# A condition vector loaded as one row and a planner's limits as a table, in an adaLN transformer block on one core

## The chip, the core and the metric

The kernel runs on one core of a Trainium2 chip. A core has five engines with queues of their own: TensorE (PE) multiplies matrices into PSUM, VectorE (DVE) and ScalarE (ACT) read PSUM and work elementwise, GpSimd (POOL) works on SBUF alone, SyncE (SP) only issues DMAs here. ACT and POOL issue DMAs too. The metric is the device time of one execution in microseconds.

## The reference

One block with adaptive layer norm: 2048 tokens, width 512, 32 heads of 16, a feed-forward part 1376 wide, all in bf16.

```python
mod = (_silu(c) @ w_mod).reshape(c.shape[0], 6, 1, -1)
sa, ca, ga, sb, cb, gb = (mod[:, i] for i in range(6))
h = _layernorm(x) * (1 + ca) + sa
q, k, v = heads(h @ wqkv)
p = _softmax(q @ k^T * Dh ** -0.5)
x = x + ga * ((p @ v) @ wo)
h = _layernorm(x) * (1 + cb) + sb
x = x + gb * (_gelu(h @ w1 + b1) @ w2 + b2)
```

(shortened; `heads` stands for the reshape and transposition into 32 heads.) The condition `c` is one row of 512. Nearly all of the time goes to the softmax: 32 x 2048 x 2048 exponentials.

## The kernel before

**Scored pairs.** The queries are cut into four blocks `b` of 512 tokens, the keys into sixteen tiles `kt` of 128, the heads into eight groups of four, a group being one `quad` with a block. A *scored pair* is one head of a quad with one key tile: a matmul of 32 rows of `kT` with 512 queries (L902, `qk`) makes 128 x 512 scores in one PSUM bank. Four heads lie on the four row groups of PE and run side by side. The last four quads are worked in two halves of 256 queries, where one pair holds two key tiles. There are 2048 pairs in all.

A pair's exponential goes one of two ways. ScalarE does two or three banks at once with Exp (L1379, `exp_to`) into `PB`. Or VectorE makes it out of integer bits: a *fill* (L1523) adds a bias and writes 16-bit integers to `TB`, which read as half floats are a piecewise power of two; two *shifts* (L1557) subtract constants, for two more pieces. Such a pair enters the second matmul three times, once with `VE` (the values) and twice with `VV`, the values scaled by `WJ[1]` and `WJ[2]`, which POOL makes at the start for six of the sixteen key tiles (L308). The second matmul (L1141, `pe_pv`) sums over all key tiles in bank 7; a column of ones gives the denominators. `emit_out` copies bank 7 out (L1472) and sends the denominators through DRAM: `d1` (L1477), back as `dall` with 16 a row (L1479), a reciprocal on VectorE (L1491), out again as `d2` (L1493), back broadcast to `rb` (L1496), and POOL multiplies (L1500). Projections, gating and the feed-forward part of the blocks run between (L435 for most of their matmuls; Gelu on ScalarE at L649 once for each of the first three blocks).

**The planner.** The order of all this work on every engine is written out by a planner that runs while the program is built. It keeps a clock for each engine, a time at which each bank and slot is free, and a due time `rdy[...]` for each result, and it asks the engine whose clock is least for its next step. What it decides is the order on each queue; on the chip an engine takes its instructions in that order and waits where an input isn't there. The limits for its choices come from `TUNE` through `tv(i)`, with one row for each 128 pairs scored (`scored[0] >> 7`), seventeen rows, all alike so far: 0, VectorE takes a further pair while the work waiting for it is under this; 1, the same for taking one outside a burst for ScalarE; 2, PE fills a bank group for ScalarE when ScalarE has less work than this ahead; 3, how far other work on PE may run over that time; 4 and 5, whether a burst waits for a bank that VectorE will soon free; 6, the least heads for which a group of second matmuls is issued early; 7, whether bank 2 is given as a third bank to ScalarE. Where PE has nothing to do the planner lets it multiply by zeros (`pe_idle`, L1222).

`open_late` (L556) is one POOL step: it frees the prologue's memory and issues the loads of `W_1` (L561) and `W_2` (L565) on ACT's queue and small ones on SP's. In `emit_out` the due time of the denominators is that of the copy plus 6000 ns (L1487); the reciprocal is placed in VectorE's order when that time has come.

**The front.** Before the planner starts, a fixed prologue runs: the first block `xb[0]` in four tiles on two queues (L140), `c` on POOL's queue spread over 128 partitions (`cc_bf`, L141: four elements on each, read one at a time), `W_m0` in two halves (L143), sixteen warm-up matmuls with zeros (`turn_over(WARM[0])`, L348), four statistics on VectorE (L353), with `W_k`'s load held until the second of them is done (L355) and SP's other loads behind it. Then come `ln_rstd`, the SiLU of `c` (`silu_c`: Exp on ScalarE, add, reciprocal and multiply on VectorE, L183 to L186), the modulation columns from `W_m0` (L231), norms, transposes (L371), evacuation to `hT` and the first projections of keys and queries (L379). `WARM[1]` isn't used.

Of the kernel before, what the change touches and what calls it, by code (L numbers as in the profile page):

```python
# [12 lines left out]
BF16 = mybir.dt.bfloat16  # L13
FP32 = mybir.dt.float32
# [6 lines left out]
P = 128  # L21
S = 2048
D = 512
F = 1376
H = 32
NC = 4
# [31 lines left out]
POOL_COVER = 1100.0  # L58
LOCK_WAIT = 100.0
TIE = 60.0  # L60
TUNE = ((1900.0, 900.0, 1350.0, 180.0, 400.0, 600.0, 3, 1),) * 17
T_NEED = 1
T_NEXT = 1
T_OPEN = 0.0
ROOT = 1000.0
ROOT_L = 700.0
SPREAD = (0.9, 0.9, 0.65)
WARM = (16, 3)
FRONT = (1200.0, 0.0, 2600.0, 4000.0)
AHEAD = 32  # L70
T_KEEP = 3
# [22 lines left out]
def adaln_block(ctx: ExitStack, tc: tile.TileContext, A_x, A_wqkv, A_wo, B_x, B_w1, B_b1, B_w2, B_b2,  # L94
                c, w_mod, out):
    nc = tc.nc
# [3 lines left out]
    const = ctx.enter_context(tc.tile_pool(name="const", bufs=1))  # L100
# [4 lines left out]
    kT = res.tile([P, NC, S], BF16, name="kT")  # L105
# [29 lines left out]
    still = kT[:, NC - 1, S - 512:S]  # L135
    nc.vector.memset(still, 0.0)
    W_m0 = prom.tile([P, NC, 2 * D], BF16, name="W_m")
    for i, eng in enumerate((nc.sync, nc.scalar)):
        for t in (2 * i, 2 * i + 1):
            eng.dma_start(out=xb[0][:, t, :], in_=x_tok[0][:, t, :])  # L140
    nc.gpsimd.dma_start(out=cc_bf, in_=c.rearrange("o (j p) -> p (o j)", p=P))  # L141
    for i, eng in enumerate((nc.sync, nc.scalar)):
        eng.dma_start(out=W_m0[:, 2 * i:2 * i + 2, :], in_=wm_v[:, 2 * i:2 * i + 2, 0:2 * D])  # L143

# [33 lines left out]
    scf = const.tile([P, NC], FP32, name="scf")  # L178
    scb = prow.tile([P, NC, P], BF16, name="scb")

    def silu_c():
        ce = const.tile([P, NC], FP32, name="ce")
        nc.scalar.activation(out=ce, in_=cc_bf, func=ACT.Exp, scale=-1.0)  # L183
        nc.vector.tensor_scalar(out=ce, in0=ce, scalar1=1.0, scalar2=None, op0=ALU.add)
        nc.vector.reciprocal(out=ce, in_=ce)
        nc.vector.tensor_tensor(out=sc_bf, in0=cc_bf, in1=ce, op=ALU.mult)  # L186
# [159 lines left out]
    def turn_over(n):  # L346
        for _ in range(n):
            nc.tensor.matmul(out=PS[0:32, 6, :], lhsT=zero, rhs=still, start=True, stop=True)  # L348

    turn_over(WARM[0])  # L350
    st0 = pron.tile([P, 12, 6], FP32, name="st1")
    for t in range(4):
        seen = nc.vector.bn_stats(out=st0[:, t, :], in_=xb[0][:, t, :])  # L353
        if t == 1:
            held = nc.sync.dma_start(out=W_k, in_=wqkv_v[:, :, D:2 * D])  # L355
            tc.add_manual_dep(held.ins, seen.ins.name, AFTER, reason="order of loads")
            nc.sync.dma_start(out=W_q, in_=wqkv_v[:, :, 0:D])
            nc.sync.dma_start(out=xb[1], in_=x_tok[1])
            nc.sync.dma_start(out=W_v, in_=wqkv_v[:, :, 2 * D:3 * D])
            for b in range(2, NQB):  # L360
                nc.sync.dma_start(out=xb[b], in_=x_tok[b])
            W_m1 = load_mod(1, nc.sync)
    psm = bk(7, FP32, 16)
    mv0, rs0 = ln_rstd(st0, 4)
    silu_c()
    first_mod_mm(psm)
    turned = [bk(2 + j, BF16) for j in range(NC)]
    for t in range(4):
# [184 lines left out]
    for j in range(NC):  # L553
        op("POOL", 1220.0, gate(lambda: W_o, j, ga_b), ("wo", j), ["ga"] + ([("wo", j - 1)] if j else []))

    def open_late():  # L556
        pro.close()
        lw = ctx.enter_context(tc.tile_pool(name="latew", bufs=1, side="right"))
        W_1 = lw.tile([P, NC, FPAD], BF16, name="W_1")
        nc.gpsimd.memset(W_1[:, :, F:FPAD], 0.0)  # L560
        nc.scalar.dma_start(out=W_1[:, :, 0:F], in_=B_w1.rearrange("(j p) n -> p j n", p=P))  # L561
        W_2 = lw.tile([P, NFC, D], BF16, name="W_2")
        lr = F - (NFC - 1) * P
        nc.gpsimd.memset(W_2[:, NFC - 1, :], 0.0)
        nc.scalar.dma_start(out=W_2[:, 0:NFC - 1, :],  # L565
                            in_=B_w2[0:(NFC - 1) * P, :].rearrange("(j p) n -> p j n", p=P))
        nc.sync.dma_start(out=W_2[0:lr, NFC - 1, :], in_=B_w2[(NFC - 1) * P:F, :])
        b1_bf = lw.tile([P, NFC], BF16, name="b1_bf")
        nc.gpsimd.memset(b1_bf, BIG)
        nc.sync.dma_start(out=b1_bf[:, 0:NFC - 1], in_=B_b1[0:(NFC - 1) * P].rearrange("(j p) -> p j", p=P))  # L570
        nc.sync.dma_start(out=b1_bf[0:lr, NFC - 1:NFC],
                          in_=B_b1[(NFC - 1) * P:F].rearrange("(p o) -> p o", o=1))
        b1c = lw.tile([P, NFC], FP32, name="b1c")
        nc.gpsimd.tensor_copy(out=b1c, in_=b1_bf)
        nc.sync.dma_start(out=W_2[lr:lr + 1, NFC - 1, :], in_=B_b2.rearrange("(o f) -> o f", o=1))
        nc.gpsimd.tensor_scalar(out=W_2[lr:lr + 1, NFC - 1, :], in0=W_2[lr:lr + 1, NFC - 1, :], scalar1=1.0 / BIG,
                                scalar2=None, op0=ALU.mult)
        clk["ACT"] += 120.0
# [883 lines left out]
    def emit_out(qi, t):  # L1462
# [21 lines left out]
            else:  # L1484
                OT[(b, ch)] = otp.tile([P, 512], BF16, name="OT")
        ot = OT[(b, ch)]
        rdy[("dall", qi)] = clk["DVE"] + 6000.0  # L1487

        def back():
            rp = osp.tile([P, 16], FP32, name="rp")  # L1490
# [254 lines left out]
```

## Time and profile before

| what | us |
|---|---|
| median of 3 timed runs (759.68 to 762.66) | 761.05 |
| the profiled execution | 759.09 |
| its span, first to last instruction | 757.2 |
| PE busy | 737.4 |
| ACT busy | 720.6 |
| DVE busy | 701.0 |
| POOL busy | 110.6 |

In the profile's rows a group reads: line, engine, operation, output <- input, shapes, count, then busy time and mean duration in ns, then the engine's idle time just before and what ended it. A timeline row begins with its start and its length in microseconds, and "x3" means three instructions merged. A row of a stretch gives its bounds and length, then busy time and count for each engine, the granted clock of TensorE as a share of full speed, the DMA engines' busy share and GB/s. A row of the chain of waits gives start, length and what the chain ran through.

### The profile page before, as it was taken

What the parts mean: (1) busy time and instruction counts of PE and PEld (TensorE: products, weight loads), DVE (VectorE), ACT (ScalarE), POOL (GpSimd) and SP (SyncE); (2) the same over time, 40 slices, a digit from 0 to 9 for tenths busy, and PEclk for the clock granted to TensorE, in tenths of its full rate; (3) what the DMA queues carried; (4) which work ended last, traced back from release to release, by engine and by line L of the source; (5) the groups of instructions that cost most, each with busy time, mean ns of one, the idle gap of its engine ahead of it and who ended that gap; (6) DMA issues with size and microseconds to landing.
All of it is one profiled execution on the core that took longest, in us unless ns stands there. A gap on an engine that the chain in (4) does not pass through costs nothing.

```text
span 757.2 us, 21449 instructions
## 1 busy us (share of the span) xinstructions
PE 737.4 (97%) x8885; PEld 259.4 (34%) x8888; DVE 701.0 (93%) x1455; ACT 720.6 (95%) x732; POOL 110.6 (15%) x137
## 2 busy tenths in 40 slices
PE   6999999999899999999999999999999999999997
PEld 3432333233233333223332232332233322444444
DVE  4966999999799999999999999999999999999984
ACT  1999999999899999999999999999999999999993
POOL 3334100211032311101001110100101110010010
PEclk8999999999999999999999999999999999999999
DMA  8300000000500100000001000000001000000000
GB/s 281 109 2 3 16 5 11 7 10 21 148 10 9 38 9 3 10 9 10 17 13 48 10 10 9 10 6 24 22 11 51 10 24 10 17 22 14 5 9 31
DMA packets 27960, 20.49 MB, mean 27 GB/s; under 512 B 14049, under 2 KB 23906, under 8 KB 27858
## 3 DMA queue, kind: packets, MB, share of 16 engines
q1 hardware_dynamic: 25442, 15.57, 7.2%
q10 hardware_dynamic: 2384, 3.51, 1.5%
q8 instruction: 71, 1.16, 0.6%
q14 instruction: 31, 0.25, 0.1%
q0 software_dynamic: 32, 0.00, 0.0%
HBM read 16.45 MB, written 2.61 MB: 25 GB/s over the span
## 4 chain that ended last, share of the span: by engine, by line
PE 64%; ACT 22%; DVE 5%; issue 5%; DMA 2%; SPq 0%; DVEq 0%; ACTq 0%
PE PS L902 22%; PE PS L1141 21%; ACT PB L1379 21%; PE PS L435 14%; PE PS L1222 3%; DVE TB L1523 3%; DVE TB L1557 2%; PE PS L770 2%; PE PS L799 1%; DMA W_m<-in_w_mod_dram 1%; DMA d<-o_sb 1%; ACT uG L649 1%; PE PS L1225 1%; PE PS L222 1%; ACT L1379 0%
## 5 line engine op out<-in xcount | busy, mean ns | idle before, releaser
L1379 ACT ACTIVATE PB<-PS 128x1024 bf16<-128x1024 f32 (+1 forms) x687 | 673.3, 1211 | 8.3 <-PE PS L902 4.6
L1523 DVE TENSOR_SCALAR TB<-PS 128x512 int16<-128x512 f32 (+1 forms) x538 | 369.5, 700 | 11.7 <-PE PS L902 9.5
L902 PE MATMUL PS<-qm,kT 32*128 32x512 bf16 (+1 forms) x2304 | 293.2, 359 | 5.4 <-ACT PB L1379 4.0
L1141 PE MATMUL PS<-PB,VE 128*32 128x512 bf16 (+1 forms) x1654 | 254.0, 361 | 0.0
L1141 PE MATMUL PS<-TB,VV 128*32 128x512 f16 (+1 forms) x1252 | 221.3, 360 | 1.8 <-DVE TB L1557 1.8
L1557 DVE TENSOR_SCALAR TB<-TB 128x1024 int16<-128x1024 int16 x556 | 219.9, 419 | 3.3
L902 PEld LDWEIGHTS <-kT 32*128 32x128 bf16 x2304 | 83.1, 91 | 253.6 <-issue 249.0
L1141 PE MATMUL PS<-TB,VE 128*32 128x512 f16 (+2 forms) x650 | 148.6, 361 | 0.2 <-DVE TB L1523 0.2
L1141 PEld LDWEIGHTS <-VE 128*32 128x32 bf16 x2304 | 72.4, 94 | 81.3 <-issue 75.3
L1222 PE MATMUL PS<-W_q,zero 128*32 128x256 bf16 x497 | 96.2, 274 | 1.3 <-DVE TB L1523 0.9
L1141 PEld LDWEIGHTS <-VV 128*32 128x32 bf16 x1252 | 57.3, 95 | 39.9 <-issue 36.6
L1222 PEld LDWEIGHTS <-zero 128*32 128x32 bf16 x497 | 46.0, 96 | 33.7 <-issue 11.1
L1500 POOL TENSOR_TENSOR OT<-o_sb,rb 128x512 bf16<-128x512 f32 (+1 forms) x16 | 19.3, 1203 | 248.4 <-DVE TB L1557 134.8
L1500 POOL TENSOR_TENSOR o_sb<-o_sb,rb 128x512 f32<-128x512 f32 (+1 forms) x16 | 19.3, 1204 | 223.4 <-DVE TB L1557 204.4
L435 PE MATMUL PS<-h2T,W 128*32 128x512 bf16 x528 | 47.3, 383 | 0.0
L435 PE MATMUL PS<-W,uG 128*32 128x512 bf16 x528 | 46.4, 383 | 0.0
L639 DVE TENSOR_SCALAR uG<-PS,b1c 128x512 bf16<-128x512 f32 x33 | 24.5, 742 | 0.0
L1503 POOL TENSOR_TENSOR OT<-OT,o_sb 128x512 bf16<-128x512 bf16 (+1 forms) x16 | 17.6, 1100 | 32.3 <-DVE TB L1557 30.1
L435 PE MATMUL PS<-W_o,OT 128*32 128x512 bf16 x272 | 22.2, 383 | 0.0
L1472 DVE COPY o_sb<-PS 128x512 f32<-128x512 f32 (+1 forms) x32 | 20.7, 647 | 0.9 <-PE PS L1141 0.8
L308 POOL TENSOR_SCALAR VV<-VE 128x512 bf16<-128x512 bf16 x12 | 18.0, 1502 | 20.7 <-DVE VE L303 12.5
L435 PE MATMUL PS<-hT,W_k 128*32 128x512 bf16 x240 | 20.9, 385 | 0.0
(124 smaller groups left out, 418.0 us busy)
## 6 DMA issues: line engine op xcount, KB each, us to landing
rb<-d SPq DMA_DIRECT2D x112, 32.0 KB
W_m<-in_w_mod_dram SPq DMA_DIRECT2D x2, 1024.0 KB
out_dram<-ob SPq DMA_DIRECT2D x16, 128.0 KB
xb<-in_A_x_dram SPq DMA_DIRECT2D x3, 512.0 KB
xr<-in_A_x_dram SPq DMA_DIRECT2D x3, 512.0 KB
W<-in_B_w_dram ACTq DMA_DIRECT2D x1, 1376.0 KB
W<-in_B_w_dram ACTq DMA_DIRECT2D x1, 1280.0 KB
W_m<-in_w_mod_dram ACTq DMA_DIRECT2D x1, 512.0 KB
```

The lines of the kernel that those rows point to most:

```text
L308: return nc.gpsimd.tensor_scalar(out=dst, in0=src, scalar1=WJ[j], scalar2=None, op0=ALU.mult)
L435: nc.tensor.matmul(out=ps[cols, :], lhsT=lhsT[:, cols], rhs=rhs, start=start, stop=stop)
L639: return lambda ps, e: nc.vector.tensor_scalar(out=T["u"][:, fc, :], in0=ps, scalar1=late["b1c"][:, fc:fc + 1], scalar2=None, op0=ALU.add)
L902: nc.tensor.matmul(out=bk(bank)[:, seg(qi, i)], lhsT=kT[32 * r:32 * r + 32, ch, kt[i] * P:(kt[i] + 1) * P], rhs=qm[(b, ch)][32 * r:32 * r ...
L1141: nc.tensor.matmul(out=PS[32 * r:32 * r + 32, 7, tok_of(qi)], lhsT=wt, rhs=src[:, seg(qi, i)], start=not started[qi][r], stop=todo[qi][r] ...
L1222: nc.tensor.matmul(out=PS[0:32, b_, 0:256], lhsT=zero, rhs=W_q[:, 0, 0:256], start=True, stop=True)
L1379: nc.scalar.activation(out=dst, in_=PS[:, b0:b0 + n, :], func=ACT.Exp, bias=-KEXP * math.log(2.0), scale=math.log(2.0) / STEP)
L1472: made = nc.vector.tensor_copy(out=o[:, cs], in_=PS[:, 7, cs])
L1500: return nc.gpsimd.tensor_tensor(out=(o if par else ot)[:, cs], in0=o[:, cs], in1=rb[:, cs], op=ALU.mult)
L1503: return nc.gpsimd.tensor_tensor(out=ot[:, cs], in0=ot[:, cs], in1=o[:, cs], op=ALU.add)
L1523: made = nc.vector.tensor_scalar(out=TB[:, u["a"]["s"], i:i + n, :], in0=PS[:, b0:b0 + n, :], scalar1=T_BIAS, scalar2=0.0, op0=ALU.add, op ...
L1557: made = nc.vector.tensor_scalar(out=TB[:, s, 0:n, :], in0=TB[:, a["s"], 0:n, :], scalar1=float(MJ[j] - MJ[j - 1]), scalar2=None, op0=ALU.add)
```

## The change

Three things are changed together. `c` is loaded as one row into one partition (into a part of `kT` that isn't in use yet), on ACT's queue ahead of the other loads; four matmuls with a single 1 turn it into columns in bank 7, and VectorE copies these to `cc_bf`. The SiLU is split into three parts, placed after the six first of now fifteen warm-up matmuls and after the first and the third of the four statistics. `TUNE` gets a row of its own for each 128 pairs. And the denominators' due time is 11000 ns behind the copy instead of 6000 where the copy is placed between 4000 ns before and 14000 ns behind POOL's clock at `open_late`.

```diff
-TUNE = ((1900.0, 900.0, 1350.0, 180.0, 400.0, 600.0, 3, 1),) * 17
+TUNE = ((1800.0, 1200.0, 1350.0, 260.0, 400.0, 600.0, 3, 1),
+        (1600.0, 900.0, 1350.0, 180.0, 400.0, 600.0, 3, 1),
+        (2400.0, 900.0, 1350.0, 180.0, 400.0, 600.0, 2, 1),
+        (1800.0, 900.0, 1350.0, 180.0, 400.0, 600.0, 4, 1),
+        (1800.0, 1200.0, 1350.0, 180.0, 400.0, 450.0, 4, 1),
+        (1800.0, 900.0, 1350.0, 220.0, 400.0, 600.0, 3, 0),
+        (1800.0, 900.0, 1350.0, 220.0, 400.0, 600.0, 4, 0),
+        (2100.0, 900.0, 1350.0, 180.0, 400.0, 600.0, 3, 1),
+        (1800.0, 1500.0, 1350.0, 180.0, 400.0, 600.0, 3, 1),
+        (1800.0, 900.0, 1350.0, 180.0, 250.0, 600.0, 2, 1),
+        (1400.0, 900.0, 1350.0, 100.0, 250.0, 600.0, 2, 1),
+        (2100.0, 900.0, 1450.0, 100.0, 250.0, 600.0, 2, 1),
+        (1700.0, 900.0, 1350.0, 180.0, 400.0, 600.0, 3, 1),
+        (1800.0, 900.0, 1350.0, 100.0, 400.0, 600.0, 3, 1),
+        (1800.0, 900.0, 1450.0, 260.0, 400.0, 450.0, 3, 1),
+        (1800.0, 900.0, 1300.0, 180.0, 400.0, 450.0, 3, 1),
+        (1800.0, 900.0, 1300.0, 180.0, 400.0, 450.0, 3, 1))
-WARM = (16, 3)
+WARM = (6, 9)
...
+    cc_row = kT[0:1, NC - 2, S - D:S]
+    one = const.tile([1, 1], BF16, name="one")
+    nc.vector.memset(one, 1.0)
+    nc.scalar.dma_start(out=cc_row, in_=c)
     for i, eng in enumerate((nc.sync, nc.scalar)):
         for t in (2 * i, 2 * i + 1):
             eng.dma_start(out=xb[0][:, t, :], in_=x_tok[0][:, t, :])
-    nc.gpsimd.dma_start(out=cc_bf, in_=c.rearrange("o (j p) -> p (o j)", p=P))
...
+    def silu_in(psm):
+        for j in range(NC):
+            nc.tensor.matmul(out=psm[:, 8 + j:9 + j], lhsT=cc_row[:, j * P:(j + 1) * P], rhs=one, start=True, stop=True)
+
+    def silu_exp(psm):
+        nc.vector.tensor_copy(out=cc_bf, in_=psm[:, 8:8 + NC])
         nc.scalar.activation(out=ce, in_=cc_bf, func=ACT.Exp, scale=-1.0)
+
+    def silu_out():
         nc.vector.tensor_scalar(out=ce, in0=ce, scalar1=1.0, scalar2=None, op0=ALU.add)
         nc.vector.reciprocal(out=ce, in_=ce)
         nc.vector.tensor_tensor(out=sc_bf, in0=cc_bf, in1=ce, op=ALU.mult)
...
     turn_over(WARM[0])
+    psm = bk(7, FP32, 16)
+    silu_in(psm)
+    turn_over(WARM[1])
     st0 = pron.tile([P, 12, 6], FP32, name="st1")
     for t in range(4):
         seen = nc.vector.bn_stats(out=st0[:, t, :], in_=xb[0][:, t, :])
-        if t == 1:
+        if t == 0:
+            silu_exp(psm)
+        elif t == 2:
+            silu_out()
+        elif t == 1:
...
-    psm = bk(7, FP32, 16)
     mv0, rs0 = ln_rstd(st0, 4)
-    silu_c()
     first_mod_mm(psm)
...
+    late_at = [0.0]
     def open_late():
...
+        late_at[0] = clk["POOL"]
...
-        rdy[("dall", qi)] = clk["DVE"] + 6000.0
+        rdy[("dall", qi)] = clk["DVE"] + (11000.0 if late_at[0] - 4000.0 <= t < late_at[0] + 14000.0 and late_at[0] else 6000.0)
```

More of the change, by code (lines that the diff above doesn't have):

```diff
@@ L60 @@
 TIE = 60.0
-TUNE = ((1900.0, 900.0, 1350.0, 180.0, 400.0, 600.0, 3, 1),) * 17
+TUNE = ((1800.0, 1200.0, 1350.0, 260.0, 400.0, 600.0, 3, 1), (1600.0, 900.0, 1350.0, 180.0, 400.0, 600.0, 3, 1), (2400.0, 900.0, 1350.0, 180.0, 400.0, 600.0, 2, 1), (1800.0, 900.0, 1350.0, 180.0, 400.0, 600.0, 4, 1), (1800.0, 1200.0, 1350.0, 180.0, 400.0, 450.0, 4, 1), (1800.0, 900.0, 1350.0, 220.0, 400.0, 600.0, 3, 0), (1800.0, 900.0, 1350.0, 220.0, 400.0, 600.0, 4, 0), (2100.0, 900.0, 1350.0, 180.0, 400.0, 600.0, 3, 1), (1800.0, 1500.0, 1350.0, 180.0, 400.0, 600.0, 3, 1), (1800.0, 900.0, 1350.0, 180.0, 250.0, 600.0, 2, 1), (1400.0, 900.0, 1350.0, 100.0, 250.0, 600.0, 2, 1), (2100.0, 900.0, 1450.0, 100.0, 250.0, 600.0, 2, 1), (1700.0, 900.0, 1350.0, 180.0, 400.0, 600.0, 3, 1), (1800.0, 900.0, 1350.0, 100.0, 400.0, 600.0, 3, 1), (1800.0, 900.0, 1450.0, 260.0, 400.0, 450.0, 3, 1), (1800.0, 900.0, 1300.0, 180.0, 400.0, 450.0, 3, 1), (1800.0, 900.0, 1300.0, 180.0, 400.0, 450.0, 3, 1))
 T_NEED = 1
@@ L179, in adaln_block @@
     scb = prow.tile([P, NC, P], BF16, name="scb")
-    def silu_c():
-        ce = const.tile([P, NC], FP32, name="ce")
+    ce = const.tile([P, NC], FP32, name="ce")
+    def silu_in(psm):
[3 more added lines that the diff above has]
+        nc.vector.tensor_copy(out=cc_bf, in_=psm[:, 8:8 + NC])
         nc.scalar.activation(out=ce, in_=cc_bf, func=ACT.Exp, scale=-1.0)
+    def silu_out():
         nc.vector.tensor_scalar(out=ce, in0=ce, scalar1=1.0, scalar2=None, op0=ALU.add)
```

## The prediction

> **What bounds the kernel now.** I read the page first: the time, the engines' shares, then the groups of instructions with their shapes kept apart.
>
> ```profile
> span 757.2 us, 21449 instructions
> PE 737.4 (97%) x8885; PEld 259.4 (34%) x8888; DVE 701.0 (93%) x1455; ACT 720.6 (95%) x732; POOL 110.6 (15%) x137
> ```
>
> ```profile
> L1379 ACT ACTIVATE PB<-PS 128x1024 bf16<-128x1024 f32 x590 | 564.6, 1152 | 2.1 <-PE PS L902 1.2 <-PE PS L1141 0.6
> L1523 DVE TENSOR_SCALAR TB<-PS 128x512 int16<-128x512 f32 x521 | 349.1, 683 | 11.7 <-PE PS L902 9.5 <-ACT PB L1379 0.3
> L1557 DVE TENSOR_SCALAR TB<-TB 128x1024 int16<-128x1024 int16 x554 | 219.4, 419 | 3.3
> L1379 ACT ACTIVATE PB<-PS 128x1536 bf16<-128x1536 f32 x96 | 151.4, 1577 | 6.2 <-PE PS L902 3.3 <-PE PS L1141 1.6 <-issue 1.3
> L1222 PE MATMUL PS<-W_q,zero 128*32 128x256 bf16 x497 | 96.2, 274 | 1.3 <-DVE TB L1523 0.9
> L1523 DVE TENSOR_SCALAR TB<-PS 128x1024 int16<-128x1024 f32 x17 | 20.6, 1214 | 0.0
> L1379 ACT ACTIVATE TB<-PS 128x1024 bf16<-128x1024 f32 x12 | 12.2, 1135 | 0.0
> ```
>
> PE at 97% isn't what bounds: 497 of its matmuls multiply by zero (L1222) to keep it warm, and a step with nothing better to do is what issues them. A scored pair's exponential goes one of two ways. ScalarE takes two or three pairs with one ACTIVATE (L1379). VectorE takes 521 + 2 x 17 = 555 pairs with a fill (L1523), then two shifts for two pairs (L1557), so about one shift a pair. The mean durations overlap from one instruction to the next, so what an instruction costs its engine is read from starts that follow one another:
>
> ```profile
> 19.12 1.45 ACT L1379 ACTIVATE PB<-PS 128x1536 bf16<-128x1536 f32 x1 [1.58 <-PE PS L902]
> ...
> 76.04 1.10 ACT L1379 ACTIVATE TB<-PS 128x1024 bf16<-128x1024 f32 x1
> 76.94 1.54 ACT L1379 ACTIVATE PB<-PS 128x1536 bf16<-128x1536 f32 x1
> 78.27 1.12 ACT L1379 ACTIVATE TB<-PS 128x1024 bf16<-128x1024 f32 x1
> ...
> 345.65 1.28 ACT L649 ACT_TABLE_LOAD   x1
> ...
> 353.16 1.02 ACT L1379 ACTIVATE PB<-PS 128x1024 bf16<-128x1024 f32 x1
> ...
> 733.27 1.28 ACT L791 ACT_TABLE_LOAD   x1
> ```
>
> ```profile
> 52.30 0.69 DVE L1523 TENSOR_SCALAR TB<-PS 128x512 int16<-128x512 f32 x1
> 52.90 0.42 DVE L1557 TENSOR_SCALAR TB<-TB 128x1024 int16<-128x1024 int16 x1
> 53.23 0.68 DVE L1523 TENSOR_SCALAR TB<-PS 128x512 int16<-128x512 f32 x1
> ```
>
> On ScalarE two pairs cost 0.90 us (76.04 to 76.94), three 1.33, so 0.45 a pair. On VectorE a fill costs 0.60 and a shift 0.33, so 0.93 a pair. ScalarE's account: from its first exponential at 19.12 to the end of the last before 733.27 are 714.2 us. Three Gelu blocks of 7.5 (345.65 to 353.16, two table loads included) take 22.5. The exponentials need 602 x 0.90 + 96 x 1.33 = 669.5. That leaves 22 us, a few evacuations included. So ScalarE is the engine that sets the time between front and tail, and a planner can win in two ways only: less of these 22 us, or pairs moved to VectorE where VectorE is idle, 0.45 us each. Where that is shows the busy time by stretches (PE, PEld, DVE, ACT, POOL, clock):
>
> ```profile
> 40.00:60.00 20.00, 19.93 (x231) 6.96 (x226) 12.87 (x25) 19.02 (x21) 6.40 (x6) 1.00 0.01 2
> 60.00:80.00 20.00, 19.90 (x236) 6.17 (x236) 15.55 (x28) 18.71 (x18) 7.38 (x5) 1.00 0.04 10
> 180.00:200.00 20.00, 16.86 (x190) 5.67 (x190) 15.66 (x32) 17.65 (x16) 3.89 (x7) 1.00 0.51 143
> 480.00:500.00 20.00, 19.13 (x203) 7.26 (x201) 17.34 (x34) 19.94 (x17) 2.44 (x2) 1.00 0.03 8
> ```
>
> VectorE is idle 7.1 and 4.4 us early, 4.3 at 180 to 200 and 2.7 at 480 to 500.
>
> **Part 1, the later due time of the denominators.** The stretch at 180 to 200 holds a stall:
>
> ```profile
> 187.81 2.02 ACTq L565 DMA_DIRECT2D W<-in_B_w_dram  x1
> 187.96 0.68 DVE L1472 COPY o_sb<-PS 128x512 f32<-128x512 f32 x1
> ...
> 198.83 0.25 DVE L1491 RECIPROCAL rp<-dall 128x16 f32<-128x16 f32 x1 [2.48 <-DMA dall<-d]
> ...
> 200.78 2.37 ACT L1379 ACTIVATE PB<-PS 128x1536 bf16<-128x1536 f32 x2 [1.75 <-PE PS L902]
> ```
>
> ```profile
> 190.58 6.48 DMA d<-o_sb
> 197.08 1.66 DMA dall<-d
> ```
>
> The output copy ends at 188.64. Its denominators go out at 190.58 behind the late weights' loads on SP, take 6.48 and 1.66 us, and land at 198.74, 10.1 us after the copy. The planner promised 6.0, so the reciprocal stood first in VectorE's order and held everything behind it for 2.48 us: fills and shifts, then through their banks PE and ScalarE (1.75 idle). With 11.0 promised the reciprocal is due after 199.6, behind 198.74. The late weights leave within 2 us of this copy, so it lies inside the new condition. What is late next is the reciprocal's row back, the gating multiplies on POOL (15% busy) and an output projection much later, so the delay costs nothing there. If that cover were gone, the five promised microseconds would show. Gain 1.8 (ScalarE's idle) to 2.5 (VectorE's), taken as **2.2**. The 2.02 us that a weight issue holds ScalarE's queue at 187.81 stays.
>
> **Part 2, the condition vector.** Removed is one POOL DMA of 0.99 us; added on ScalarE's queue one DMA, ahead of two x tiles and half of W_m; on PE four one-column matmuls between six and nine warm-up matmuls (15 instead of 16); on VectorE one small copy after the first statistics, with the three SiLU operations after the third instead of after the fourth.
>
> ```profile
> 0.73 0.88 ACTq L140 DMA_DIRECT2D xb<-in_A_x_dram  x2
> 1.21 5.12 PE L348 MATMUL PS<-kT,zero 128*32 128x512 bf16 x16 [1.21 <-DVE kT L136]
> 1.24 0.99 POOL L141 DMA_DIRECT2D cc_bf<-in_c_dram  x1 [0.81 <-POOLq L1728]
> ...
> 3.61 2.52 DVE L353 BATCH_NORM_STATS2 st<-xb 128x6 f32<-128x512 bf16 x4
> 4.97 0.37 SPq L355 DMA_DIRECT2D W_k<-in_A_wqkv_dram  x1
> ...
> 9.30 0.16 DVE L186 TENSOR_TENSOR sc_bf<-cc_bf,ce 128x4 bf16<-128x4 bf16 x1
> ...
> 10.74 0.99 PE L231 MATMUL PS<-sc_bf,W_m 128*128 128x1 bf16 x32 [4.41 <-DMA W_m<-in_w_mod_dram]
> ...
> 13.77 0.10 PEld L379 LDWEIGHTS <-W_q 128*128 128x128 bf16 x1 [0.48 <-DMA W_q<-in_A_wqkv_dram]
> ```
>
> SiLU is ready at 9.46 now and was never what PE waited for: W_m ended the wait at 10.74, W_q the next one at 13.77. The earlier vector therefore buys **0.0**. Both ends: one more issue of 0.44 (half of 0.88) ahead of half of W_m can cost 0.44, and POOL free 0.99 sooner lets the masks and statistics begin sooner and W_k with them, which can bring W_q at most its 0.48 earlier. The new wait is VectorE's copy on PE's four matmuls on the DMA. Behind it stand three statistics, W_k's load with all of SP's loads behind it, and the norms. A small row took 1.66 us on a free queue and 6.48 behind weights; issued at 0.73 it lands near 2.4 to 3, or in the bad case near 7.2. The warm-up's first six (0.32 each) end at 3.1, so in the first case the copy is done about when the first statistics end; in the second W_k leaves some 3 us late and the front loses up to that. I take the first: nothing else is in the queue ahead of it.
>
> The clock in this stretch is one more term:
>
> ```profile
> 14.00:16.00 2.00, 1.78 (x5) 0.73 (x5) 0.17 (x1) 0.72 (x2) 0.00 (x0) 0.50 1.09 348
> ```
>
> ```profile
> 14.58 2.77 PE PS L379 x6
> ```
>
> PE idles 4.4 us from the warm-up's end to 10.74 and the projections run at a granted clock of 0.50: six in 2.77, so at 1.0 all eight would be 1.8 us shorter. The nine warm-ups after the vector end later only if the vector is late, so I leave this stretch as it is.
>
> [...]
>
> **Part 3, the table.** Every row differs from (1900, 900, 1350, 180, 400, 600, 3, 1), so the whole order is dealt anew; no instruction is added but through the share of VectorE's pairs and the zero matmuls. Bounds: below nothing, if the rows fit this chip worse than the uniform one (the third case); above, all of ScalarE's 22 us less the 2.2 already counted. Between them I go by the holes that VectorE shows. The 2.7 us at 480 to 500 are room for 2.7 / 0.93 = 2.9 pairs, 1.3 us of ScalarE. The 11.5 us at 40 to 80 are room for 12.4 pairs, 5.6 us. Half of these can't be had by limits: a pair may go to VectorE only where its key tile's scaled values exist, and POOL makes the last four of those as late as 63.3 to 69.3:
>
> ```profile
> 63.31 6.00 POOL L308 TENSOR_SCALAR VV<-VE 128x512 bf16<-128x512 bf16 x4 [1.85 <-DVE VE L303]
> ```
>
> So 2.8 + 1.3 = **4.1**.
>
> **Sum.** 2.2 + 0.0 + 4.1 = 6.3 us. The profiled execution took 759.09 (1.9 around its span of 757.2), so it would become 752.8. The median of the three runs is 761.05, 2.0 above the profiled one; on that scale the forecast is 761.05 - 6.3 = **754.8**.
>
> **The rivals.**
>
> *Only the stall goes.* VectorE's early holes are POOL's, elsewhere the engines are full, and what one row gains the next gives back. For it: outside the four stretches quoted no hole of size shows. Against it: the 22 us of ScalarE are spread wider than the stall. Time: 761.05 - 2.2 = 758.9.
>
> *Slower: pairs go back to ScalarE.* The first limit says with how much work waiting VectorE still takes a pair. Thirteen of the seventeen rows lower it, one to 1400, where VectorE already idles at 480 to 500. If that costs 5% of the pairs in 13/17 of the run, 555 x 0.05 x 0.76 = 21 pairs x 0.45 = 9.5 us; less 2.2 it is +7.3, so 768.3. It decides from 2.2 / 0.45 = 5 lost pairs on. For it: ScalarE has no room. Against: rows 2, 7 and 11 raise the limit, and VectorE at 93% can take only what it has time for, whatever the limit.
>
> *The clock stays up in the front.* The forecast with 1.8 us more off: 753.0. For it: the nine warm-ups come later than the last nine of the sixteen. Against: the wait for W_m is unchanged and 4.4 us long.
>
> **How the numbers follow.** The forecast has 0.56, only the stall 0.14, pairs back 0.25, the clock 0.05. The measurement can't tell less than 0.5%, 3.8 us, from no change: faster is below 757.2, same up to 764.9. The forecast and the clock case are faster (0.61), the stall alone is same (0.14), pairs back is slower (0.25). The likeliest case's own range is 747 to 757.2: from 14 us off, two thirds of ScalarE's slack, to 3.8 off. The whole range has to reach into the third case: 746 to 766.
>
> **What would show it.** Part 1: no idle VectorE ahead of L1491 near the late weights, though their transfers are as slow; wrong if the reciprocal still waits over 1 us. Part 2: SiLU ready near 6.5, yet W_m still ends PE's wait near 10.7 and the first exponential stays within 0.6 of 19.12; wrong if it moves by over 1 us. Part 3: more than 555 pairs on VectorE, some 15 more, and VectorE idle less than 11.5 us from 40 to 80; a count of 550 or less says the third case. The forecast is wrong as a whole if the first-to-last exponential takes as long as now.

## The result and the profile after

| | median us | runs |
|---|---|---|
| before, on the same chip | 761.34 | 4 (759.68 to 762.66) |
| after | 750.15 | 4 (749.82 to 750.67) |

The ratio is 0.9856 with a 95% interval of 0.984 to 0.9872: the change makes the kernel 11.2 us faster. The forecast was 754.8, so the direction was right and the time lies in the range, but the gain is nearly twice the 6.3 us of the sum, and a good part of it comes from a place that the prediction priced at nothing.

The page of the profiled execution (749.94 us, 1.7 more than its span):

```profile
span 748.2 us, 21318 instructions
PE 730.9 (98%) x8836; PEld 253.8 (34%) x8839; DVE 702.6 (94%) x1436; ACT 719.8 (96%) x728; POOL 110.4 (15%) x136
```

The groups with shapes kept apart (the lines have moved: L1379 is L1398 now, L1523 is L1542), and the first and the last end of ScalarE's exponentials in its timeline:

```profile
L1398 ACT ACTIVATE PB<-PS 128x1024 bf16<-128x1024 f32 x580 | 558.4, 1165 | 2.8 <-PE PS L921 0.9 <-DMA W<-in_B_w_dram 0.9 <-PE PS L1160 0.7
L1542 DVE TENSOR_SCALAR TB<-PS 128x512 int16<-128x512 f32 x472 | 316.4, 687 | 7.2 <-PE PS L921 5.4
L1398 ACT ACTIVATE PB<-PS 128x1536 bf16<-128x1536 f32 x101 | 160.0, 1584 | 1.1 <-PE PS L921 1.0
L1542 DVE TENSOR_SCALAR TB<-PS 128x1024 int16<-128x1024 f32 x42 | 51.2, 1219 | 0.9 <-PE PS L921 0.6
L1398 ACT ACTIVATE TB<-PS 128x1024 bf16<-128x1024 f32 x14 | 13.6, 1064 | 0.0
```

```profile
14.46 1.45 ACT L1398 ACTIVATE PB<-PS 128x1536 bf16<-128x1536 f32 x1 [1.05 <-PE PS L921]
...
723.53 1.28 ACT L810 ACT_TABLE_LOAD   x1
```

With the prediction's way of cutting the time, the 9.0 us between the two profiled spans are: 4.66 in the front (first exponential at 14.46 instead of 19.12), 5.08 from there to the end of the last exponential (709.07 instead of 714.15), and 0.74 lost in the tail (24.67 instead of 23.93). VectorE takes 472 + 2 x 42 = 556 pairs, one more than before. So ScalarE's exponentials need as long as they did: 594 x 0.90 + 101 x 1.33 = 668.9 us (669.5 before). Less these and 22.5 for the Gelu blocks, 17.7 us of slack (time in which ScalarE isn't kept busy at that price) are left of 709.07, where 22.1 were left before.

The front, in the timeline:

```profile
5.83 0.16 DVE L197 TENSOR_TENSOR sc_bf<-cc_bf,ce 128x4 bf16<-128x4 bf16 x1
...
7.74 0.90 PE L242 MATMUL PS<-sc_bf,W_m 128*128 128x1 bf16 x30 [0.97 <-DMA W_m<-in_w_mod_dram]
8.61 1.38 DVE L228 TENSOR_SCALAR xb<-xb,mv,rs 128x512 bf16<-128x512 bf16 x4 [1.49 <-POOL rs L220]
...
11.32 0.10 PEld L395 LDWEIGHTS <-W_q 128*128 128x128 bf16 x1 [0.99 <-DMA W_q<-in_A_wqkv_dram]
```

W_m still ends PE's wait, but at 7.74 instead of 10.74, and the projections from W_q come at 11.32 instead of 13.77. W_m isn't what limits the front any longer. In the chain of waits, first of before, then of after:

```profile
1.68 9.01 DMA W_m<-in_w_mod_dram
```

```profile
1.69 4.44 DMA xb<-in_A_x_dram
...
7.53 1.05 POOL rs L220
...
8.61 0.42 DVE xb L228
...
11.55 1.46 PE PS L395 x6
```

Before, the chain waits for W_m until 10.69; now it goes through the last tile of x, its statistics and the norms. The DMA engines show why W_m can come sooner. First two stretches of one microsecond of before, then of after (the last two columns are the DMA engines' busy share and GB/s):

```profile
4.00:5.00 1.00, 1.00 (x5) 0.44 (x4) 1.00 (x3) 0.00 (x0) 1.00 (x14) 1.00 0.66 166
...
7.00:8.00 1.00, 0.00 (x0) 0.00 (x0) 0.00 (x0) 0.00 (x0) 0.92 (x3) 1.00 0.50 126
```

```profile
4.00:5.00 1.00, 1.00 (x7) 0.43 (x6) 0.84 (x3) 0.21 (x1) 1.00 (x10) 1.00 1.00 380
...
7.00:8.00 1.00, 0.27 (x10) 0.27 (x11) 0.12 (x2) 0.00 (x0) 0.70 (x2) 1.00 1.01 342
...
12.00:13.00 1.00, 1.00 (x6) 0.34 (x5) 0.00 (x0) 0.17 (x1) 0.00 (x0) 1.00 1.10 354
```

Before, with nothing but large loads and the 1 KB of the condition vector under way, the DMA engines were busy half of the time from 7 to 8 us and moved 126 GB/s; now they move at least 342 in every microsecond from 4 to 8. And from 12 to 13 us the granted clock is 1.00 where it was 0.50. From W_q to the first exponential it takes 3.14 us now, 5.35 before; six of the projections take 1.46 us instead of 2.77 (they start 0.21 to 0.22 us apart at the clock of 1.00, 0.42 to 0.43 at 0.50). So the front's 4.66 us are 2.45 of an earlier start of the projections and 2.2 of a shorter way from there, most of it the clock.

The stall at the late weights, on VectorE and on ScalarE:

```profile
182.90 0.68 DVE L1491 COPY o_sb<-PS 128x512 f32<-128x512 f32 x1
...
197.32 0.24 DVE L1510 RECIPROCAL rp<-dall 128x16 f32<-128x16 f32 x1
```

```profile
181.71 1.49 ACTq L583 DMA_DIRECT2D W<-in_B_w_dram  x1
183.25 27.44 ACT L1398 ACTIVATE PB<-PS 128x1024 bf16<-128x1024 f32 x27 [0.92 <-DMA W<-in_B_w_dram]
```

The reciprocal comes 13.7 us behind the end of its copy and waits for nothing; ScalarE runs through 27 exponentials where it stood for 1.75 us. They start about 1.01 us apart and not 0.90 as in the account above, so slack can hide in time that the profile shows as busy. The 1.49 us of a weight's issue on ScalarE's queue are still there.

### The profile page after: what moved, and what is told of

The parts are those of the page before. It is cut to its first block, busy times and chain, and to the rows that moved or that the text cites. A ratio compares the mean times of both kernels' runs of the same rounds, so it can differ in the third digit from the quotient of the medians.

```text
span 748.2 us, 21318 instructions
## 1 busy us (share of the span) xinstructions
PE 730.9 (98%) x8836; PEld 253.8 (34%) x8839; DVE 702.6 (94%) x1436; ACT 719.8 (96%) x728; POOL 110.4 (15%) x136
## 4 chain that ended last, share of the span: by engine, by line
PE 58%; ACT 32%; issue 4%; DVE 3%; DMA 1%; ACTq 0%; POOL 0%; DVEq 0%
ACT PB L1398 31%; PE PS L921 20%; PE PS L1160 19%; PE PS L451 11%; PE PS L1241 3%; DVE TB L1542 2%; PE PS L789 1%; PE PS L818 1%; PE PS L1244 1%; ACT uG L668 1%; PE PS L233 1%; DVE TB L1576 1%; DMA xb<-in_A_x_dram 1%; ACT L1398 0%; PE PS L395 0%
## 5 line engine op out<-in xcount | busy, mean ns | idle before, releaser
L1398 ACT ACTIVATE PB<-PS 128x1024 bf16<-128x1024 f32 (+1 forms) x681 | 670.7, 1227 | 3.8 <-PE PS L921 2.0
L1542 DVE TENSOR_SCALAR TB<-PS 128x512 int16<-128x512 f32 (+1 forms) x514 | 367.3, 730 | 8.1 <-PE PS L921 6.1
L921 PE MATMUL PS<-qm,kT 32*128 32x512 bf16 (+1 forms) x2304 | 294.7, 358 | 4.9 <-ACT PB L1398 3.1
L1160 PE MATMUL PS<-PB,VE 128*32 128x512 bf16 (+1 forms) x1646 | 249.4, 361 | 1.1 <-DVE o_sb L1491 1.1
L1576 DVE TENSOR_SCALAR TB<-TB 128x1024 int16<-128x1024 int16 (+1 forms) x558 | 221.5, 423 | 4.6
L921 PEld LDWEIGHTS <-kT 32*128 32x128 bf16 x2304 | 82.9, 91 | 254.9 <-issue 248.9
L1160 PE MATMUL PS<-TB,VE 128*32 128x512 f16 (+2 forms) x658 | 147.0, 361 | 0.3 <-DVE TB L1542 0.2
L1241 PE MATMUL PS<-W_q,zero 128*32 128x256 bf16 x408 | 80.4, 273 | 2.2 <-DVE TB L1542 1.2
L1241 PEld LDWEIGHTS <-zero 128*32 128x32 bf16 x408 | 37.3, 96 | 27.7 <-issue 8.7
L451 PE MATMUL PS<-h2T,W 128*32 128x512 bf16 x528 | 45.5, 383 | 0.0
L1244 PE MATMUL PS<-W_q,zero 128*32 128x256 bf16 x101 | 22.2, 275 | 0.0
```

Source lines behind the costliest of these rows:

```text
L451: nc.tensor.matmul(out=ps[cols, :], lhsT=lhsT[:, cols], rhs=rhs, start=start, stop=stop)
L921: nc.tensor.matmul(out=bk(bank)[:, seg(qi, i)], lhsT=kT[32 * r:32 * r + 32, ch, kt[i] * P:(kt[i] + 1) * P], rhs=qm[(b, ch)][32 * r:32 * r ...
L1160: nc.tensor.matmul(out=PS[32 * r:32 * r + 32, 7, tok_of(qi)], lhsT=wt, rhs=src[:, seg(qi, i)], start=not started[qi][r], stop=todo[qi][r] ...
L1241: nc.tensor.matmul(out=PS[0:32, b_, 0:256], lhsT=zero, rhs=W_q[:, 0, 0:256], start=True, stop=True)
L1244: nc.tensor.matmul(out=PS[32 * o_:32 * o_ + 32, 7, c_:c_ + 256], lhsT=zero, rhs=W_q[:, 0, 0:256], start=False, stop=False)
L1398: nc.scalar.activation(out=dst, in_=PS[:, b0:b0 + n, :], func=ACT.Exp, bias=-KEXP * math.log(2.0), scale=math.log(2.0) / STEP)
```

## The experiments

All times are medians, each beside the kernel before run on the same chip. Differences between two of these kernels are of medians too, some of them from different chips, on which the kernel before took 760.52 to 761.34.

| kernel | median us | before | ratio and interval |
|---|---|---|---|
| front_only | 756.65 | 761.08 | 0.9946 (0.9928 to 0.9963) |
| due_only | 757.77 | 761.08 | 0.9957 (0.9941 to 0.9974) |
| table_only | 759.67 | 761.08 | 0.9985 (0.9973 to 0.9997) |
| no_due (front, table) | 755.60 | 761.08 | 0.9936 (0.9916 to 0.9955) |
| front_due | 754.88 | 761.16 | 0.9922 (0.9908 to 0.9936) |
| flat_1800 | 752.82 | 761.16 | 0.989 (0.9871 to 0.9909) |
| table_reversed | 761.83 | 761.16 | 1.0016 (1.0004 to 1.0028) |
| late_on_sp | 753.71 | 761.16 | 0.9916 (0.9896 to 0.9937) |
| extra_cols | 751.78 | 760.52 | 0.9884 (0.9858 to 0.991) |
| extra_row | 750.50 | 760.52 | 0.9872 (0.9847 to 0.9897) |
| cols_on_act | 759.79 | 760.52 | 0.9987 (0.9972 to 1.0002) |
| warm_34 | 759.83 | 760.52 | 0.9988 (0.9975 to 1.0001) |

### Each part alone, and all but one

front_only: the changed kernel with both planner edits undone.

```diff
-TUNE = ((1800.0, 1200.0, 1350.0, 260.0, 400.0, 600.0, 3, 1), ...
+TUNE = ((1900.0, 900.0, 1350.0, 180.0, 400.0, 600.0, 3, 1),) * 17
...
-        rdy[("dall", qi)] = clk["DVE"] + (11000.0 if late_at[0] - 4000.0 <= t < late_at[0] + 14000.0 and late_at[0] else 6000.0)
+        rdy[("dall", qi)] = clk["DVE"] + 6000.0
```

> The kernel before with the condition vector's row, the split SiLU and the split warm-up alone; limits uniform and due times as before, so the order behind the front is that of before. In the traces of before and after the first exponential went from 19.12 to 14.46 us, the stretch from there to the end of the last one from 714.15 to 709.07, and the tail from 23.9 to 24.7. Theory A (the terms add up): first exponential at about 14.5, the rest as before, 4.7 us faster (about 756.6). Theory B (the front's gain needs the new order behind it): the rest grows by what the front wins, and it comes out within 2 us of before.

Measured: 4.4 us faster. Theory A. But its profiled execution was the slowest of six (759.99; the others 756.42 to 758.41), and it shows what the profile of before had not. First exponential in ScalarE's timeline, then VectorE, then ScalarE at the stall:

```profile
16.31 1.45 ACT L1398 ACTIVATE PB<-PS 128x1536 bf16<-128x1536 f32 x1 [1.43 <-PE PS L921]
```

```profile
197.21 0.25 DVE L1510 RECIPROCAL rp<-dall 128x16 f32<-128x16 f32 x1 [4.37 <-DMA dall<-d]
```

```profile
199.15 2.41 ACT L1398 ACTIVATE PB<-PS 128x1536 bf16<-128x1536 f32 x2 [3.64 <-PE PS L921]
202.91 1.02 ACT L1398 ACTIVATE PB<-PS 128x1024 bf16<-128x1024 f32 x1 [1.34 <-PE PS L921]
```

And the stretches behind it (PE, PEld, DVE, ACT, POOL, clock):

```profile
196.00:198.00 2.00, 0.21 (x3) 0.10 (x3) 0.79 (x3) 0.00 (x0) 1.74 (x2) 1.00 0.02 7
...
202.00:204.00 2.00, 2.00 (x13) 0.49 (x12) 1.69 (x3) 1.02 (x1) 0.00 (x0) 0.50 0.02 2
```

The wait for the denominators is 4.37 us here instead of 2.48, PE has next to nothing to do from 194 to 198, and from about 199 the granted clock is 0.50. From 202 to 204 PE works all the time and ScalarE only 1.02 of 2.00 us; its waits end with PE's scores (L921), which fits scores that come later at the lower clock: in the chain of waits a piece of them takes 0.53 to 0.61 us from 199.83 on, and 0.33 at 198.78, when the clock was still at 1.00. From the first to the last exponential this execution takes 717.48 us, 3.3 more than the profiled execution of before with the same planner limits. So the stall has a second price here, and not every execution pays one: the profiled one of before waited 2.48 us and kept its clock (1.00 in every stretch from 186 to 206).

In these traces PE's idle stretch comes first, but neither its length nor that of the 0.50 is the same everywhere. Here PE works 0.50 of the 4 us from 194 to 198, and the 0.50 lasts 6.8 us (199.3 to 206.1 by the stretches); in table_only PE works 1.36 of the same 4 us, and the 0.50 lasts 3.4 us; in extra_cols below it begins near 9.1 us, behind only some 2 us in which PE is mostly idle. What sets these lengths was not shown.

due_only: the kernel before with `late_at` and the longer due time.

> The kernel before with the longer due time of the denominators alone. Theory A: VectorE no longer waits ahead of the reciprocal at 180 to 200 us, and the time falls by 1.8 to 2.5 us (to about 759). Theory B (ScalarE's 2 us behind a weight issue and slow transfers set this stretch, and the stall only moves): within 0.8 us of before. The changed due time deals the order anew behind this place, which may add or take a microsecond.

Measured: 3.3 us faster, more than A's upper end; B falls. The 0.8 us over that end fit the clock: its runs show a mean granted clock of 0.994 to 0.998, those of before 0.987 to 0.993. The order behind the stall is another one as well (628 double exponentials instead of 602), and the two weren't separated. In its profile the reciprocal doesn't wait.

table_only: the kernel before with the table.

> The kernel before with the table of limits alone. Theory A: first exponential at 19.1, the stall of 2.5 us ahead of the reciprocal at 180 to 200 us stays in some form, and the rest wins what the two traces leave for the table, 5.1 less 2.0 to 2.5, so about 3 us faster (758.5). Theory B (the table fits only an order with the longer due time): no gain, within 1 us of before, or slower. The count of pairs on VectorE stays at about 555 in both; a table that wins by more pairs on VectorE would show some 10 more.

Measured: 1.4 us faster, the interval just short of no change; between the theories. VectorE took 554 pairs: VectorE's share didn't grow, in this kernel as in the changed one.

no_due: the changed kernel with 6000 for all.

```diff
-        rdy[("dall", qi)] = clk["DVE"] + (11000.0 if late_at[0] - 4000.0 <= t < late_at[0] + 14000.0 and late_at[0] else 6000.0)
+        rdy[("dall", qi)] = clk["DVE"] + 6000.0
```

> The changed kernel with the due time back at 6000 for all. Theory A (the terms add up): 2 us slower than the changed kernel, so 752.2, with VectorE idle about 2.5 us ahead of a reciprocal near 190 us. Theory B (the table's rows were found with the longer due time and lose their fit without it): more than 4 us slower, above 754.

Measured: 755.6, which is 5.4 us slower than the changed kernel: B by its number. Its six runs say more than their median. Time, and mean granted clock:

```
752.32 0.999    755.23 0.997    755.33 0.997
755.88 0.994    755.98 0.994    758.47 0.992
```

The lower the clock, the longer the time, within one and the same program; only the fastest of the six was profiled, so where the others lost their clock isn't shown. table_only and no_due have the same planner limits behind different fronts, and their profiled executions differ in this as well. The stretch behind the stall, first table_only (its reciprocal waited 2.99 us), then no_due (1.31 us):

```profile
198.00:200.00 2.00, 2.00 (x17) 0.99 (x14) 1.86 (x5) 1.02 (x1) 0.00 (x0) 0.50 0.14 43
```

```profile
198.00:200.00 2.00, 2.00 (x28) 0.67 (x26) 2.00 (x5) 2.00 (x3) 0.10 (x1) 1.00 0.00 0
```

From the first to the last exponential they take 714.75 and 712.18. The changed kernel's four runs lie within 0.9 us of each other, with clocks of 0.996 to 0.999, so with the stall gone the spread is smaller too. That isn't so in every kernel: flat_1800 below has no such stall in its profile, and its runs lie 3.3 us apart.

### What made the front faster

extra_cols: the changed kernel, with the old load added and its result unused.

```diff
+    cc_x = const.tile([P, NC], BF16, name="cc_x")
+    nc.gpsimd.dma_start(out=cc_x, in_=c.rearrange("o (j p) -> p (o j)", p=P))
```

> The changed kernel with the old load of the condition vector added: 512 elements of two bytes on POOL's queue, at its old place, into a tile that nothing reads. Theory A (the scattered two-byte load holds up the large loads that share the DMA engines): W_m ends PE's wait at 9.5 to 11 us again instead of 7.7, the first exponential moves from 14.5 to 17 or later, and the kernel loses 2.5 to 5 us. Theory B (SiLU's place in the order and the earlier start of POOL's and VectorE's work won the front): W_m at 7.5 to 8.0 and the time within 0.6 us of the changed kernel's 750.2.

extra_row: the same with one row.

```diff
+    nc.gpsimd.dma_start(out=kT[0:1, NC - 3, S - D:S], in_=c)
```

> The changed kernel with a load of the condition vector as one row on POOL's queue added, at the place of the old load, into a row that nothing reads. Theory A (the two-byte elements are what costs, not the queue): W_m at 7.5 to 8.2 and the time within 0.8 us of the changed kernel. Theory B (a transfer that POOL issues costs, whatever its shape): as with the scattered load, W_m at 9.5 or later and 2.5 us or more lost. In both POOL's clearing starts 1 us later, which nothing in the front waits for by more than a few tenths.

cols_on_act: the kernel before with its load moved to the other kind of queue.

```diff
-    nc.gpsimd.dma_start(out=cc_bf, in_=c.rearrange("o (j p) -> p (o j)", p=P))
+    nc.scalar.dma_start(out=cc_bf, in_=c.rearrange("o (j p) -> p (o j)", p=P))
```

> The kernel before with its scattered load of the condition vector issued on ScalarE's queue instead of POOL's. Theory A (the two-byte elements): W_m still ends PE's wait at 9.5 us or later, the time within 1.5 us of before (761.1). Theory B (POOL's queue): W_m below 8.5 and about 3 us or more faster.

The columns from W_m on PE, one row each for extra_cols, extra_row and cols_on_act:

```profile
9.27 0.96 PE L244 MATMUL PS<-sc_bf,W_m 128*128 128x1 bf16 x30 [1.69 <-DMA W_m<-in_w_mod_dram]
```

```profile
7.87 0.90 PE L243 MATMUL PS<-sc_bf,W_m 128*128 128x1 bf16 x30 [0.87 <-DMA W_m<-in_w_mod_dram]
```

```profile
9.65 1.18 PE L231 MATMUL PS<-sc_bf,W_m 128*128 128x1 bf16 x32 [3.26 <-DMA W_m<-in_w_mod_dram]
```

With one scattered load of 1 KB that nobody reads, W_m comes at 9.27 instead of 7.74, the clock falls to 0.50, the first exponential comes at 17.34, and the median is 1.6 us longer (751.78; 1.3 longer than extra_row on the same chip); a row on the same POOL queue does nothing (750.50); with the scattered load on ScalarE's queue W_m still comes as late as 9.65. 9.27 is less than theory A's 9.5, and the loss less than its 2.5, so the sizes were set too high.

W_m's landing also varies by itself: with a row alone 7.5 to 9.1 in the profiles of eight kernels, with the scattered load 9.3 to 10.7 in five whose PE waited for it. So one landing time alone doesn't prove much, but the rates of the DMA engines do. The lower rate of the two stretches 4 to 6 and 6 to 8 us, and the rate in the first slice of the page (18.7 to 19.0 us long):

| vector loaded | GB/s, two microseconds | GB/s, first slice |
|---|---|---|
| scattered, POOL's queue (before, due_only, table_only, warm_34, extra_cols) | 180 to 210 | 275 to 289 |
| scattered, ScalarE's queue (cols_on_act) | 151 | 287 |
| as a row only | 351 to 360 (after, front_only, no_due, extra_row) | 310 to 313 (all eight) |

So it is the scattered shape, not the queue, that holds up the large loads. Whether its two-byte elements or its 128 partitions do it wasn't separated, and in what way it holds them up is not shown.

How much of the 4.4 us of front_only this load explains stays open: put back into the changed kernel it costs 1.3 to 1.6. The rest lies in what else the front changes, above all SiLU, or in the different order behind it; no run separates them. SiLU's new place belongs to the gain in any case: before, the vector landed so late (ScalarE's Exp waits for it until 8.64) that SiLU was ready only at 9.46, and with W_m at 7.74 PE would have waited for SiLU instead. Nor does the row always keep the clock up: with it the clock still read 0.50 in the front of front_only (first exponential at 16.31) and of flat_1800 (17.38).

warm_34: the kernel before with `WARM = (34, 3)`.

> The kernel before with 34 warm-up matmuls instead of 16, so that PE has work until about 10 us. W_m's landing isn't touched (9.6 to 10.7 in the runs so far). Theory A (PE's idle time ahead of W_m is what halves the granted clock from 11 to 18 us): the clock stays at 1.00 in the front, the projections take 0.21 us each instead of 0.43, and the first exponential comes about 2 us earlier (16.5 to 17), so about 759. Theory B (the clock falls in this stretch for what runs there, small matmuls and waits for hT, not for the idle time before): the clock reads 0.50 from 12 to 16 us again and the time stays within 0.6 us of before.

In stretches and on ScalarE:

```profile
12.00:14.00 2.00, 1.48 (x11) 0.70 (x9) 0.99 (x2) 1.45 (x2) 0.00 (x0) 1.00 1.10 350
...
196.00:198.00 2.00, 1.20 (x10) 0.30 (x9) 1.97 (x5) 0.00 (x0) 0.47 (x1) 0.50 0.08 12
...
204.00:206.00 2.00, 2.00 (x17) 0.40 (x12) 1.48 (x4) 1.49 (x2) 0.00 (x0) 0.50 0.01 4
```

```profile
16.04 1.45 ACT L1379 ACTIVATE PB<-PS 128x1536 bf16<-128x1536 f32 x1 [1.05 <-PE PS L902]
```

Theory A for the mechanism: with PE at work until W_m is there the clock stays at 1.00 and the first exponential comes at 16.04, with W_m's columns no earlier than 10.36: 5.7 us behind them instead of 8.4 before. For the time both missed: 759.83, 0.7 us faster, the interval touching no change. The profile shows where the gain went: at the stall near 195 us the clock falls to 0.50 for about 10 us, and the stretch between first and last exponential takes 717.34. What the front wins can be paid back at the stall.

### The table

front_due: the changed kernel with the uniform limits of before.

> The changed kernel with the uniform limits of before: front and longer due time, no table. So far, in medians against 761.1: front alone -4.4, due time alone -3.3, table alone -1.4, front and table -5.5, all three -10.9. Theory A (the terms add up): -7.7, so 753.4, and the table is worth 3.2 on top of it. Theory B (front and due time need each other: an earlier front alone lengthens the stall at 190 to 200 us, which halves the clock there): clearly more than -7.7, 751.5 or less, and the table is worth 1.4 on top, as alone. In the trace VectorE doesn't wait ahead of the reciprocal, and the clock stays at 1.00 from 190 to 210 us.

Measured: 754.88, 6.3 us faster: neither number is met, the sum of the two parts alone (7.7) being nearer. Its reciprocal near 197 us still waits 0.52, and the clock stays at 1.00 there. The table is worth 4.7 on top of it, 1.4 alone.

table_reversed: row 15 first, row 0 last.

> The changed kernel with the rows of the table in the opposite order (row 15 first), all else as changed. Theory A (the rows fit the stretches they were found for): the table's gain is lost and more, 754 or slower, at or behind the uniform limits. Theory B (any change of limits deals the order anew, and rows of this kind are as good anywhere): within 1.5 us of the changed kernel's 750.2.

Measured: 761.83, 11.7 us slower than the changed kernel and slower than the kernel before. Theory A, and by more than it said. VectorE takes 556 pairs here too. Part of the loss is that the stall is back in spite of the longer due time (VectorE, and the clock from 180 to 200):

```profile
193.14 0.25 DVE L1510 RECIPROCAL rp<-dall 128x16 f32<-128x16 f32 x1 [3.40 <-DMA dall<-d]
```

```profile
180.00:200.00 20.00, 17.14 (x171) 5.05 (x167) 15.43 (x31) 15.75 (x16) 3.58 (x6) 0.83 0.53 151
```

But two of its runs with a clock of 1.000 take 760.47 and 761.66, so most of it lies elsewhere; where was not shown.

flat_1800: all rows as before, but 1800 for the first limit.

```diff
-TUNE = ((1900.0, 900.0, 1350.0, 180.0, 400.0, 600.0, 3, 1),) * 17
+TUNE = ((1800.0, 900.0, 1350.0, 180.0, 400.0, 600.0, 3, 1),) * 17
```

> The changed kernel with uniform limits whose first is 1800 instead of 1900, the value that eight of the seventeen rows have. Theory A (stretch by stretch is what wins): within 1 us of the uniform limits of before with front and due time, so 752.5 to 754.5. Theory B (the table wins by its base of 1800): within 1 us of the changed kernel's 750.2.

Measured: 752.82, in A's range but 2.1 us faster than front_due and 2.7 slower than the changed kernel. So the table's base of 1800 may have some of the table's 4.7 us, and the rows the rest; with four runs from 751.74 to 755.05 this split is rough. The slowest of them is the profiled one, with its late front (17.38); the two with a clock of 1.000 took 751.74 and 752.11, which would leave the rows less than 2 us. (1800 stands in eleven of the seventeen rows, not in eight.)

late_on_sp: the two late weights on SP's queue.

```diff
-        nc.scalar.dma_start(out=W_1[:, :, 0:F], in_=B_w1.rearrange("(j p) n -> p j n", p=P))
+        nc.sync.dma_start(out=W_1[:, :, 0:F], in_=B_w1.rearrange("(j p) n -> p j n", p=P))
...
-        clk["ACT"] += 120.0
```

(and the same for `W_2`)

> The changed kernel with the loads of the two late weights on SP's queue instead of ScalarE's, and the planner's 120 ns for them on ScalarE taken away. ScalarE's queue was held 1.49 us by the second of these loads at 181.7 us in the changed kernel (2.02 in the one before), and its next exponential began 0.92 us late. Theory A: ScalarE and PE win these 0.9 to 1.9 us, so about 749. Theory B (SP's queue then sends the denominators out 2 us later, and the reciprocal waits again in spite of its longer due time): the same or slower, with VectorE idle ahead of the reciprocal near 197 us.

SP's queue, then VectorE, then all engines from 180 to 200:

```profile
181.04 3.97 SPq L585 DMA_DIRECT2D W<-in_B_w_dram  x1
...
185.53 4.32 SPq L589 DMA_DIRECT2D b_bf<-in_B_b_dram  x1
```

```profile
195.19 0.25 DVE L1509 RECIPROCAL rp<-dall 128x16 f32<-128x16 f32 x1 [0.60 <-DMA dall<-d]
```

```profile
180.00:200.00 20.00, 18.97 (x217) 6.42 (x210) 19.40 (x40) 19.84 (x21) 2.51 (x5) 1.00 0.51 151
```

By its time this is theory B, by its mechanism it isn't. In its own place the edit does what theory A said: ScalarE is busy 19.84 of 20 us there (19.08 in the changed kernel). SP's queue is held for 8 us and the reciprocal waits 0.60, much less than theory B needs. Yet the kernel is 3.6 us slower. From the first to the last exponential it takes 714.35 instead of 709.07, and VectorE has 553 pairs instead of 556: the 120 ns taken off the planner's clock dealt everything behind that place anew. That the table's fit was lost with the new order is the likely cause; it wasn't separated from the move of the loads.

## Why the prediction came out as it did

**What bounds the kernel: right.** ScalarE's exponentials need 669 to 670 us in every order tried, and what changes is the slack around them. By the same account the slack is 22.1 us before, 21.7 in front_due, 17.7 after and 30.4 in table_reversed (14.29 to 735.95, 579 double and 111 triple exponentials).

**Part 1, the due time: right mechanism, too small.** The term was 2.2; alone it measured 3.3, and 5.4 on top of front and table. The rows quoted were the direct stall of one execution, the one in which the clock stayed at 1.00. In the profiles of table_only, front_only, warm_34 and table_reversed (waits of 2.99 to 4.37 us) the clock then reads 0.50 for 3 to 10 us, and on the page of cols_on_act (3.2 us) it is down to 0.8 in the slice from 189 to 208; with a wait of 1.31 us in no_due it stays at 1.00. The step "Gain 1.8 (ScalarE's idle) to 2.5 (VectorE's)" took one execution's stall for its price; the median of before, 2.0 above its profiled run, was the hint.

**Part 2, the condition vector: this step failed.** "The earlier vector therefore buys **0.0**" took W_m's landing as given, and let the new load cost at most 0.44 and win at most 0.48. What it priced at nothing is what the removed load did to the others: W_m came 3.0 us sooner, and the first exponential moved by 4.66 where over 1 us was named as the sign of being wrong. The part measured 4.4 us alone, of which the load put back takes 1.3 to 1.6. SiLU's moment was no matter only as long as W_m was late. The rows to see it in were there, 126 GB/s and half-idle DMA engines from 7 to 8 us, but the prediction asked only who waited for the vector. The last rival, the clock staying up, came true in the changed kernel's profile with some 2.2 us (1.8 forecast). The rows put it down to W_m and not to the nine warm-ups: these end 0.3 us later than before, while PE's longest wait ahead of W_m's columns is 0.97 us instead of 4.41. The first six warm-ups start 0.43 us apart and not 0.32, so the vector was in columns at 4.16, and VectorE stood 0.59 for it; W_k's load left at 4.95 all the same (4.97 before). "W_m still ends PE's wait near 10.7" was wrong.

**Part 3, the table: nearly the size, another mechanism.** 4.1 was forecast; 4.7 was measured on top of front and due time, 1.4 alone. But "some 15 more" pairs on VectorE did not come: 556 against 555. VectorE's hole at 480 to 500 did close, and the one at 40 to 80 shrank (8.8 us idle, 11.6 before), yet the pairs gained there were given back elsewhere. The stretches of after:

```profile
40.00:60.00 20.00, 20.00 (x241) 6.88 (x243) 12.77 (x23) 19.04 (x21) 7.02 (x5) 1.00 0.01 1
60.00:80.00 20.00, 19.87 (x248) 5.84 (x236) 18.39 (x36) 20.00 (x21) 6.17 (x5) 1.00 0.04 11
480.00:500.00 20.00, 19.35 (x219) 6.90 (x219) 19.68 (x40) 19.94 (x17) 1.67 (x2) 1.00 0.04 9
```

The gain is less slack on ScalarE at an equal share, so that 4.1 and 4.7 lie close together is luck.

**The rivals.** Pairs back to ScalarE didn't happen; its sum counts thirteen rows that lower the first limit, and there are fourteen, which would make it 10.3 us instead of 9.5. Only the stall went is excluded by front_only, 4.4 us faster with the stall still there. table_reversed shows that the slower outcome was possible by another way than the one forecast: no pairs lost, more slack.

**Sum.** Measured alone, part 2 gives 4.4 us more than its term, part 1 gives 1.1 more and part 3 2.7 less: 9.1 instead of 6.3. Together the parts make 11.2, so the terms don't add up. Front and due time are worth less with each other (6.3 instead of 7.7). Table and longer due time are worth more, which fits a table found for that order; that it was found so was not shown. That the time lies in the range in spite of a term priced at nothing is owed to the range's width, 20 us.

What stays open: which of the seventeen rows wins what, whether the base of 1800 alone has the 2.1 us, and what in the front has the part of its gain that the scattered load doesn't explain. A load of the scattered kind is also left in both kernels: `open_late` brings a bias of 2.5 KB in elements of two bytes (`b_bf`) on SP's queue, beside the late weights and just ahead of the denominators. From 188 to 190 us of before the DMA engines move 169 and 229 GB/s, then 290 or more until 197; whether that load lengthens the stall wasn't tried.

## What to carry to other kernels

A small load is priced by what it does to the loads beside it as well as by who waits for it: look at the GB/s and the busy share of the DMA engines while it is under way (here 126 GB/s and 0.50 from 7 to 8 us of before, 342 and 1.01 after). A stall in which TensorE ran dry cost more here than its own length: in front_only 4.37 us of waiting were followed by 6.8 us at a clock of 0.50, in the profile of before 2.48 us by none. So a profile of one execution can show the smaller half; the spread of the runs and their mean clock tell. And a planner's tuned limits belong to one order of work: an edit that moves its clocks by little can cost the fit (likely in late_on_sp), so tune last.

## What was not expected of the hardware

- 1 KB loaded as 512 elements of two bytes over 128 partitions held up the large loads beside it: 126 GB/s from 7 to 8 us of before against 342 after, and 151 to 210 over two microseconds against 351 or more without it; and W_m landed at 9.3 to 10.7 us instead of 7.5 to 9.1, whether POOL's or ScalarE's queue issued it.
- The same program's executions differ by up to 6 us (no_due, 752.32 to 758.47), the longer ones with the lower mean clock (0.999 to 0.992); a stretch at half clock shows as ScalarE's idle time (1.02 busy of 2.00 in front_only).
- Issuing a DMA held a queue for 0.37 to 0.53 us for most in the front of after, but 1.49 and 2.02 on ScalarE's queue for the second of two late weights, and 3.97 and 4.32 on SP's behind them in late_on_sp.
